# Gated recurrence with top-80 routing to eight experts: last loads on 128 partitions, zero writes in quarters, experts' products alternating, scatters without a chain

## The chip, the core and the metric

One core of a Trainium2 chip runs the whole program. Its engines are TensorE (PE in the rows; PEld is its weight load), VectorE (DVE), ScalarE (ACT), GpSimd (POOL) and SyncE (SP, which here only issues transfers); 16 DMA engines move data. The metric is device time in microseconds (us), the median of several executions. "The profiled execution" is one of them, and its span runs from its first to its last instruction.

## What is computed

Inputs are `x` and `f_logit` of shape (4, 5056, 256), a `lower_bound` of 256 values, `w_gate` (256, 8), `w1` (8, 256, 1024), `w2` (8, 1024, 256) and a capacity of 80; all are float32. Cut to what matters:

```python
sig = 1.0 / (1.0 + np.exp(-f_logit))
f = lower_bound + (1.0 - lower_bound) * sig
for t in range(S):                       # S = 5056, for each of 4 batches
    h = f[:, t] * h + (1.0 - f[:, t]) * x[:, t]
    y[:, t] = h
x = y.reshape(20224, 256)                # the tokens
logits = x @ w_gate                      # 8 experts
expert_idx = np.argmax(logits, axis=1)
gate_w = softmax(logits)[np.arange(N), expert_idx]
out = np.zeros((N, D))
for e in range(8):
    tok_idx = the (at most) 80 tokens of expert e with the largest gate_w
    h = np.maximum(x[tok_idx] @ w1[e], 0.0)
    out[tok_idx] = gate_w[tok_idx, None] * (h @ w2[e])
```

So 640 rows of the output hold values, and all others are zero.

## The kernel before, in words

**Stream.** The 5056 steps of a batch are cut into ten groups of 512 (the tenth has 448). A unit `n` is one batch of one group: 40 units, four to a group, batch by batch. For a unit, SP loads `f_t` and `x_t` (512 KB each; 448 KB on 112 partitions in the last group); ACT makes the sigmoid (`gate`); POOL multiplies it into `x_t` (`enter`); PE transposes both into channels by time (`to_channels`, tiles `sp` and `up`); ACT turns `sp` into the decay in the SBUF tensor `h_all` (`decay`); DVE runs the recurrence over time (`scan`, two halves of 128 channels); PE makes the gate logits (`lg`). The tile `up` has three PSUM buffers, of which a unit takes two. Once in four units a group's logits are copied (`aside`, `ls`), turned to tokens by PE (`lt`) and reduced by DVE (`maxima`, tiles `mx` and `cand`, then `choice`, tiles `eq` and `pick`). The loop over `n` issues the load of unit n+3, the gate of n+2, the transposes of n+1, the scan of n and the logits of n-1. Each engine works through its own list in the order in which the code was written.

**Zeros.** A 1 MB block of zeros in DRAM (`z_dram`) is copied over the output by SP. `clear` writes a piece; `zeros` lists the 160 pieces of 16 rows (128 KB; the last 8 have 96 KB). From unit 4 to unit 31 two pieces follow each unit's loads; 16 follow the last load, 40 go between and behind the first weights, 48 go with later weights.

**Selection.** After the stream every expert's candidates are reduced on all engines to a list of tokens (`vals`, `rank`, `put`, `kept`), which ends in `trow`, the token numbers.

**Experts.** Weights come in halves of 512 KB into a ring of six (`wring`); six halves are loaded ahead, the rest as halves are used up (`more`). For each expert, `gather` copies 80 columns of `h_all`, each by an instruction whose address comes out of a register: 24 on DVE, 32 on ACT, 24 on POOL, after one load of registers from `trow` per engine. `scaled` (tile `xt`), `hidden` (PE, `h_ps`), `relu` (ACT, `hid`), `result` (PE, `y_ps`), `finish` (DVE, `y`) follow, each for a whole expert. On PE the eight chunks of `hidden` for one expert stand ahead of the eight chunks of `result` for the one before it.

**Scatter.** `scatter` writes the 80 rows of `y` by an indirect DMA from POOL. All eight wait until the zero writes have landed, since they overwrite zeros, and each waits for the one before it to land, since both write `out`. SP's DMAs take eight semaphores in turn, so that each waits for the DMA eight places earlier to land.

The branch behind `doubt` (a full selection for rare ties) is not taken with these inputs.

Of the kernel before, what the change touches and what calls it, by code (L numbers as in the profile page):

```python
# [11 lines left out]
I32 = mybir.dt.int32  # L12
U32 = mybir.dt.uint32
# [4 lines left out]
P = 128  # L18
TOP = 8
AWAY = 1.0e6  # L20
PAD = 104
NONE = -64.0
GONE = -1.0e4
STEP = 128.0


@with_exitstack
def kernel(
# [25 lines left out]
    BESIDE = 4  # L54
# [13 lines left out]

    def tiles(ap, b, g):
        return ap[b, ds(first(g), size(g))].rearrange("(p r) d -> p r d", r=R)  # L70

    W = P // R
    assert B == R and C == R * R and all(size(g) % C == 0 for g in range(n_grp))
# [47 lines left out]
    NEW = DEEP + (n_grp - OLD) * P  # L121
# [3 lines left out]
    tops = consts.tile([P, NP, TOP], F32, name="tops")  # L125
    prev = consts.tile([P, 2 * TOP], F32, name="prev")
# [12 lines left out]
    h_all = hpool.tile([P, DC, N], F32, name="h_all")  # L139
# [8 lines left out]
    ZQ = 8  # L148
# [4 lines left out]
    def clear(k, q=None):  # L153
        n = min(ZR, N // P - k) * D
        rows = slice(0, P) if q is None else ds(q * QP, QP)
# [12 lines left out]
    def tokens(pool, at, ids):  # L168
# [5 lines left out]
        nc.vector.tensor_scalar(ids, parts[:, 0], float(S - R * W), spot_of[:, 0:1],  # L174
# [9 lines left out]
    psu = psum.enter_context(tc.tile_pool(name="psu", bufs=3, space=PSUM))  # L184
    plg = psum.enter_context(tc.tile_pool(name="plg", bufs=1, space=PSUM))

    with tc.tile_pool(name="ld", bufs=4) as ld, \
# [3 lines left out]

        def spot(n):
            g, b = divmod(n, B)
            return b * S + first(g)
# [40 lines left out]
        def load_f(n):  # L235
            g, b = divmod(n, B)
            fs[n] = ld.tile([P, R, D], F32, name="f_t", tag="f_t")
            nc.sync.dma_start(
                out=fs[n][:run(g)], in_=tiles(f_logit, b, g))

        def load_x(n):
            g, b = divmod(n, B)
            xs[n] = ld.tile([P, R, D], F32, name="x_t", tag="x_t")
            nc.sync.dma_start(
                out=xs[n][:run(g)], in_=tiles(x, b, g))

        def gate(n):
            s_t = sts[n] = fs.pop(n)[:run(n // B)]
            nc.scalar.activation(s_t, s_t, ACT.Sigmoid, scale=-1.0)  # L249

        def enter(n):
            u_t = uts[n] = xs.pop(n)[:run(n // B)]
            (nc.gpsimd if n else nc.vector).tensor_tensor(u_t, sts[n], u_t, ALU.mult)  # L253

        def to_channels(n, src, dst, pool, tag, in_time):
            k = run(n // B)
            for o in range(DC):
                ps = pool.tile([P, G], F32, name=tag, tag=tag)
                for r in range(R):
                    at = ps[:, r:R * k:R] if in_time else ps[:, ds(r * k, k)]  # L260
                    nc.tensor.transpose(at, src[n][:, r, ds(o * P, P)], ident[:k, :k])  # L261
                dst[n, o] = ps[:, :R * k]
            del src[n]

        def columns(n, o):
            return h_all[:, o, ds(spot(n), size(n // B))]
# [576 lines left out]
```

## Time and profile before

| | |
|---|---|
| median of 3 executions | 262.93 us (260.38 to 266.25) |
| the profiled execution, its own time | 260.38 us |
| its span | 258.6 us |
| busy: PE, DVE, ACT, POOL | 193.7, 160.7, 136.6, 136.4 us |
| moved by DMA | 81.13 MB, mean 314 GB/s |

Busy shares are means over stages with different limits, so the program has to be read stage by stage: the stream up to about 142 us, the selection up to about 163 us, the experts up to about 234 us, and the last scatters after that.

### The profile page before, as it was taken

Reading aid. Unit: us, or ns where it says so; the run is one execution under the profiler, and the core shown is the slowest. Engines: PE = TensorE matmul, PEld = TensorE weight load, DVE = VectorE, ACT = ScalarE, POOL = GpSimd, SP = SyncE. Lnnn points to the kernel's source line nnn. Section 1 sums busy time; section 2 is a strip of 40 time slices with the busy share of each in tenths; the row PEclk is TensorE's granted clock in tenths of the full one; section 3 lists DMA queues with packets and bytes.
Section 4 is the critical chain, followed back from the end, with each engine's and each line's share of the span. In section 5 each row is a group of like instructions: output and inputs, shape, how many; then the busy total and the mean of one; then the engine's idle time right before and its main releaser. Section 6 shows DMA issues by size and latency. Waiting matters only on the chain.

```text
span 258.6 us, 6254 instructions
## 1 busy us (share of the span) xinstructions
PE 193.7 (75%) x1841; PEld 159.1 (62%) x1841; DVE 160.7 (62%) x430; ACT 136.6 (53%) x430; POOL 136.4 (53%) x279
## 2 busy tenths in 40 slices
PE   1879989898889898988486758979999888882000
PEld 1757777676767676766364558868888657651000
DVE  4566988989898989897638488457555335000000
ACT  3657877676778787866744315465666551100000
POOL 2457878777777777776473710457444400012221
PEclk9997999999999999999979579999999999999555
DMA  6999999999999999999965888769999999961010
GB/s 190 402 418 416 421 415 426 414 416 417 420 414 415 418 414 420 414 370 274 297 212 161 286 273 297 205 202 340 324 351 371 345 354 362 326 249 35 20 31 15
DMA packets 30811, 81.13 MB, mean 314 GB/s; under 512 B 5040, under 2 KB 13360, under 8 KB 28336
## 3 DMA queue, kind: packets, MB, share of 16 engines
q1 hardware_dynamic: 29840, 79.97, 84.1%
q0 software_dynamic: 384, 0.66, 0.9%
q8 instruction: 17, 0.28, 0.4%
q14 instruction: 26, 0.21, 0.2%
q10 hardware_dynamic: 544, 0.01, 0.1%
HBM read 78.91 MB, written 22.41 MB: 392 GB/s over the span
## 4 chain that ended last, share of the span: by engine, by line
DMA 37%; PE 23%; DVE 12%; issue 8%; ACT 8%; SPq 6%; POOL 3%; ACTq 1%; POOLq 0%; DVEq 0%
DMA w_sb<-in_moe_w_dram 11%; DMA f_t<-in_f_logit_dram 10%; DMA x_t<-in_x_dram 8%; DVE h_all L278 6%; PE up L261 5%; PE h_ps L673 5%; PE sp L261 5%; DMA out_dram<-y,goal 5%; SPq L156 5%; PE lg L292 3%; ACT h_all L271 3%; PE y_ps L688 3%; DMA wg<-in_moe_w_gate_dram 2%; DVE eq L328 2%; ACT xe L655 2%
## 5 line engine op out<-in xcount | busy, mean ns | idle before, releaser
L253 POOL TENSOR_TENSOR x_t<-f_t,x_t 128x1024 f32<-128x1024 f32 (+1 forms) x39 | 92.3, 2369 | 32.6 <-DMA x_t<-in_x_dram 22.6
L278 DVE TENSOR_TENSOR_SCAN h_all<-h_all,up 128x512 f32<-128x512 f32 (+1 forms) x80 | 94.8, 1242 | 9.3 <-PE up L261 6.0
L249 ACT ACTIVATE f_t<-f_t 128x1024 f32<-128x1024 f32 (+1 forms) x40 | 42.4, 1059 | 31.9 <-DMA f_t<-in_f_logit_dram 31.9
L261 PE MATMUL up<-ident,x_t 128*128 128x128 f32 (+1 forms) x320 | 47.0, 287 | 13.6 <-DVE h_all L278 7.6
L271 ACT ACTIVATE h_all<-sp,nomlb 128x512 f32<-128x512 f32 (+1 forms) x80 | 49.9, 673 | 6.5 <-PE sp L261 6.3
L261 PE MATMUL sp<-ident,f_t 128*128 128x128 f32 (+1 forms) x320 | 46.0, 289 | 7.3 <-ACT f_t L249 5.8
L261 PEld LDWEIGHTS up<-ident,x_t 128*128 128x128 f32 (+1 forms) x320 | 37.2, 147 | 18.9 <-DVE h_all L278 8.4
L261 PEld LDWEIGHTS sp<-ident,f_t 128*128 128x128 f32 (+1 forms) x320 | 36.4, 147 | 15.8 <-issue 13.0
L655 POOL COPY xe<-h_all 128x2 f32 x192 | 23.9, 187 | 22.6 <-DVE xt L662 8.8
L655 ACT COPY xe<-h_all 128x2 f32 x256 | 25.4, 190 | 14.1 <-issue 10.6
L688 PE MATMUL y_ps<-w_sb,hid 128*80 128x256 f32 x128 | 29.3, 381 | 4.4 <-DMA w_sb<-in_moe_w_dram 2.9
L673 PE MATMUL h_ps<-xt,w_sb 128*128 128x80 f32 x256 | 30.0, 276 | 3.5 <-DMA w_sb<-in_moe_w_dram 1.8
L673 PEld LDWEIGHTS h_ps<-xt,w_sb 128*128 128x128 f32 x256 | 29.2, 192 | 5.1 <-PE y_ps L688 1.9
L292 PE MATMUL lg<-h_all,wg 128*32 128x128 f32 (+1 forms) x640 | 27.3, 288 | 6.1 <-ACT ls L300 4.5
L655 DVE COPY xe<-h_all 128x2 f32 x192 | 22.6, 172 | 12.5 <-issue 12.5
L697 POOL DMA_INDIRECT out_dram<-y,goal x8 | 7.5, 938 | 42.5 <-DMA w_sb<-in_moe_w_dram 25.8
L688 PEld LDWEIGHTS y_ps<-w_sb,hid 128*80 128x80 f32 x128 | 18.5, 150 | 13.0 <-ACT hid L681 4.8
L292 PEld LDWEIGHTS lg<-h_all,wg 128*32 128x32 f32 x640 | 15.8, 110 | 13.4 <-ACT ls L300 6.4
L694 DVE TENSOR_SCALAR y<-y_ps,gsl 80x256 f32<-80x256 f32 x8 | 3.8, 479 | 24.0 <-PE y_ps L688 24.0
L681 ACT ACTIVATE hid<-h_ps 128x320 f32<-128x320 f32 x16 | 6.6, 431 | 17.4 <-PE h_ps L673 17.4
L166 PEld LDWEIGHTS warm<-ident 128*128 128x128 f32 x92 | 12.5, 220 | 0.1
L166 PE MATMUL warm<-ident 128*128 128x128 f32 x92 | 12.5, 302 | 0.0
(125 smaller groups left out, 101.1 us busy)
## 6 DMA issues: line engine op xcount, KB each, us to landing
out_dram<-z_dram SPq DMA_DIRECT2D x152, 128.0 KB, 5.8
f_t<-in_f_logit_dram SPq DMA_DIRECT2D x36, 512.0 KB, 6.2
x_t<-in_x_dram SPq DMA_DIRECT2D x36, 512.0 KB, 6.2
w_sb<-in_moe_w_dram SPq DMA_DIRECT2D x32, 512.0 KB, 5.7
f_t<-in_f_logit_dram SPq DMA_DIRECT2D x4, 448.0 KB, 8.4
x_t<-in_x_dram SPq DMA_DIRECT2D x4, 448.0 KB, 9.7
z_dram<-zero SPq DMA_DIRECT2D x1, 1024.0 KB, 9.1
out_dram<-z_dram SPq DMA_DIRECT2D x8, 96.0 KB, 5.4
```

The source lines that it names most:

```text
L156: nc.sync.dma_start(out=out_z[rows, ds(k * D, n)], in_=z_dram[rows, :n])
L166: nc.tensor.matmul(warm, ident, ident, start=True, stop=True)
L249: nc.scalar.activation(s_t, s_t, ACT.Sigmoid, scale=-1.0)
L253: (nc.gpsimd if n else nc.vector).tensor_tensor(u_t, sts[n], u_t, ALU.mult)
L261: nc.tensor.transpose(at, src[n][:, r, ds(o * P, P)], ident[:k, :k])
L271: nc.scalar.activation(columns(n, o).rearrange("c (p r) -> c p r", r=R), sps.pop((n, o)).rearrange("c (r p) -> c p r", r=R), ACT.Identity, ...
L278: nc.vector.tensor_tensor_scan(h, h, ups.pop((n, o)), h_all[:, o, ds(spot(n) - 1, 1)] if n >= B else 0.0, ALU.mult, ALU.add)
L292: nc.tensor.matmul(lgs[g][ds(r * LC, LC), b, :k], wg[:, o], h[:, r], start=o == 0, stop=o == DC - 1, skip_group_check=True)
L655: copy(X[e][:, :, ds(k + j, 1)], h_all[:, :, ds(v, 1)])
L673: nc.tensor.matmul(h_ps[:, c], halves[i][:, o, ds(c * P, P)], xt[:, o], start=o == 0, stop=o == DC - 1, skip_group_check=True)
L688: nc.tensor.matmul(y_ps, hid[:, c], halves[c // CH][:, c % CH], start=c == 0, stop=c == FC - 1)
L697: nc.gpsimd.indirect_dma_start(out=out, out_offset=bass.IndirectOffsetOnAxis(ap=goal[:, ds(e, 1)], axis=0), in_=Y.pop(e), in_offset=None, ...
```

## The change

**Layout.** `h_all` becomes (batch, half, time), so that one batch's two halves lie 5056 columns apart. `trow` then holds byte addresses (4 times the column plus `HOME`, the address of `h_all`), and `rows_of` adds five small DVE operations that turn column numbers into output rows.

**Loads.** In the last group a load takes the last 512 steps of the batch (64 of them a second time) on 128 partitions; gate, product and transposes run on all 512, decay and scan on the new 448. The last unit's work is no longer moved ahead of its place. `up` gets four buffers; the selection's `ct` uses the buffers of `sp`.

**Zeros.** Pieces are quarters (32 rows, 256 KB), and neighbouring ones go out as one DMA of up to 1 MB: 14 in the loop, 6 after the last load, 30 among the first six weight halves, 30 with later ones (20 of 26 halves).

**Selection.** The second half of the early groups is summed on DVE (`sums`, `worth` on DVE for groups 6 and 7) instead of POOL; all 64 early maxima go into `fresh`, so that the last reductions are 320 wide instead of 268 and the reduction of the early ones alone goes; 16 warming matmuls go.

**Experts.** `gather` copies a token's two values as 2 x 4 bytes from a byte address, with no register arithmetic ahead of each copy (before: one register instruction ahead of each copy of 2 floats); 34 on DVE and 28 on ACT in two parts each, 18 on POOL; one `xt` product instead of two; on PE a chunk of `hidden` and the chunk of `result` six steps back alternate; weights come by halves in the order in which they are used.

**Scatter.** The scatters are declared independent of each other.

```diff
-        return ap[b, ds(first(g), size(g))].rearrange("(p r) d -> p r d", r=R)
+        return ap[b, ds(first(g) - lead(g), G)].rearrange("(p r) d -> p r d", r=R)
...
-    ZQ = 8
+    ZQ = 4
...
     def clear_some(m):
-        for k, q in zeros[:m]:
-            clear(k, q)
-        del zeros[:m]
+        while m > 0 and zeros:
+            k, q = zeros[0]
+            n = min(m, ZQ - q)
+            clear(k, q, n)
+            del zeros[:n]
+            m -= n
...
-    psu = psum.enter_context(tc.tile_pool(name="psu", bufs=3, space=PSUM))
+    psu = psum.enter_context(tc.tile_pool(name="psu", bufs=4, space=PSUM))
...
             if n + AHEAD == LAST:
-                clear_some(2 * ZQ)
-            elif B <= n < n_unit - 2 * B:
-                clear_some(2)
+                clear_some(6)
+            elif B <= n < n_unit - 2 * B and n % 2:
+                clear_some(1)
...
+        halved(0, HALF)
+        sums(HALF, OLD)
+        worth(0, 0, 2, nc.gpsimd)
+        candidates(0)
+        worth(OLD - 2, HALF, 2, nc.vector)
+        aside(g)
...
+    LAG = FC - 2
+    order = sorted(((which, e, i) for which in (1, 2) for e in range(E) for i in range(2)),
+                   key=lambda k: e_step(k, FC, CH, LAG))
+    RING = 6
...
-    for key in order[:3]:
+    for key in order[:RING]:
         w_sb[key] = weights(*key)
-        clear_some(ZQ)
-    clear_some(len(zeros) - BESIDE * (E - 2) * 2)
+        clear_some(5)
...
-    ways = [(mybir.EngineType.DVE, nc.vector.tensor_copy, 24),
-            (mybir.EngineType.Activation, nc.scalar.copy, 32),
-            (mybir.EngineType.Pool, nc.gpsimd.tensor_copy, K - 56)]
+    ways = [(mybir.EngineType.DVE, nc.vector.tensor_copy, [18, 16]),
+            (mybir.EngineType.Activation, nc.scalar.copy, [14, 14]),
+            (mybir.EngineType.Pool, nc.gpsimd.tensor_copy, [K - 62])]
...
+    h_bytes = h_all.rearrange("p b o s -> p (b o s)").bitcast(U8)
...
-                for o in range(DC):
-                    nc.vector.tensor_scalar_mul(XT[e][:, o], x_e[:, o], omlb[:, ds(o, 1)])
+                nc.vector.tensor_tensor(XT[e], X.pop(e),
+                                        omlb.unsqueeze(2).broadcast_to([P, DC, K]), ALU.mult)
...
-                    clear_some(BESIDE)
+                    clear_some(1 + len(late) % 2)
...
+            def steps(lo, hi):
+                for s in range(lo, hi):
+                    if s < E * FC:
+                        hidden(s)
+                    if 0 <= s - LAG < E * FC:
+                        result(s - LAG)
...
+                for other in sent:
+                    tc.declare_no_dep(one.ins, other.ins,
+                                      reason="a token is in one expert's list only")
+                sent.append(one)
...
+            for e in range(E):
+                s = e * FC
+                gather(e + 2, (0,))
+                steps(s, s + CH)
+                relu(e, 0)
+                gather(e + 2, (1,))
+                steps(s + CH, s + LAG)
+                if e > 0:
+                    finish(e - 1)
+                    scatters(e - 1)
+                elif not again:
+                    settle()
+                scaled(e + 2)
+                steps(s + LAG, s + FC)
+                relu(e, 1)
```

On SP the end of the stream stands like this before: loads of the last group, zero pieces (16 rows each) and the first weights.

```order
L238 DMA f_t<-in_f_logit_dram 112x1024
L244 DMA x_t<-in_x_dram 112x1024 x2
L156 DMA out_dram<-z_dram 16x2048 x16
L500 DMA w_sb<-in_moe_w_dram 128x2x512 x2
L156 DMA out_dram<-z_dram 16x2048 x8
L504 DMA w_sb<-in_moe_w_dram 128x4x256 x2
```

And like this after:

```order
L246 DMA f_t<-in_f_logit_dram 128x1024
L248 DMA x_t<-in_x_dram 128x1024
L164 DMA out_dram<-z_dram 64x2048
L164 DMA out_dram<-z_dram 128x2048
L490 DMA w_sb<-in_moe_w_dram 128x2x512
L164 DMA out_dram<-z_dram 128x2048
L164 DMA out_dram<-z_dram 32x2048
L490 DMA w_sb<-in_moe_w_dram 128x2x512
```

The same bytes of zeros take fewer and larger DMAs, and the weights go in one half at a time.

On POOL the last scatters stand like this before, with their waits (DMASW is the landing of an earlier scatter, DVE the tile `y`):

```order
L697 DMA out_dram<-y,goal 20224x256 [waits DMASW3_49,DVE_49]
L697 DMA out_dram<-y,goal 20224x256 [waits DMASW4_49,DVE_49]
L697 DMA out_dram<-y,goal 20224x256 [waits DMASW5_49,DVE_49]
L697 DMA out_dram<-y,goal 20224x256 [waits DMASW6_49,DVE_49]
```

And all eight like this after (DMAHW is the landing of the zeros and loads):

```order
L734 DMA out_dram<-y,goal 20224x256 [waits DMAHW4_49,DMAHW5_49,DMAHW3_49,DMAHW6_49,DMAHW2_49,DMAHW7_49,DMAHW1_49,DMAHW0_49]
L734 DMA out_dram<-y,goal 20224x256 x2
L734 DMA out_dram<-y,goal 20224x256 [waits DVE_49] x5
```

The first still waits for the zeros; none waits for another scatter.

## Rows read from the trace of the kernel before

**Rows 1.** Busy by stretch (PE, PEld, DVE, ACT, POOL), granted clock, DMA share, GB/s.

```profile
98.35:110.80 12.45, 10.93 (x140) 8.93 (x136) 11.43 (x13) 9.50 (x13) 9.56 (x6) 1.00 1.02 418
...
114.60:126.50 11.90, 9.91 (x126) 7.86 (x124) 10.14 (x13) 8.69 (x13) 5.79 (x3) 1.00 1.04 267
...
139.00:162.50 23.50, 16.53 (x141) 13.78 (x135) 16.95 (x59) 6.90 (x24) 8.04 (x21) 0.78 0.84 274
162.50:174.00 11.50, 9.04 (x77) 8.70 (x78) 6.73 (x53) 7.14 (x67) 6.22 (x50) 1.00 0.67 192
...
204.00:229.90 25.90, 21.55 (x142) 17.68 (x143) 7.48 (x54) 6.54 (x46) 0.13 (x2) 1.00 1.00 350
```

**Rows 2.** Timeline of DVE: start, length, operation, idle before it and its releaser.

```profile
33.38 0.29 DVE L318 TENSOR_REDUCE mx<-lt 128x16 f32<-128x128 f32 x1 [1.50 <-PE lt L306]
...
108.10 0.29 DVE L318 TENSOR_REDUCE mx<-lt 128x16 f32<-128x128 f32 x1 [0.95 <-PE lt L306]
108.42 0.29 DVE L319 TENSOR_TENSOR cand<-lt,mx 128x128 f32<-128x128 f32 x1
...
112.55 0.29 DVE L332 TENSOR_REDUCE pick<-eq 128x16 f32<-128x128 f32 x1
...
139.15 0.27 DVE L328 SCALAR_TENSOR_TENSOR eq<-cand,revexp 128x128 f32<-128x128 f32 x1
...
139.66 2.18 DVE L278 TENSOR_TENSOR_SCAN h_all<-h_all,up 128x448 f32<-128x448 f32 x2
```

**Rows 3.** Groups by line from 60 to 110 us: busy, mean ns, idle before.

```profile
L278 DVE TENSOR_TENSOR_SCAN h_all<-h_all,up 128x512 f32<-128x512 f32 x33 | 39.5, 1259 | 0.0
...
L261 PE MATMUL up<-ident,x_t 128*128 128x128 f32 x128 | 18.2, 277 | 4.0 <-DVE h_all L278 4.0
...
L328 DVE SCALAR_TENSOR_TENSOR eq<-cand,revexp 128x128 f32<-128x128 f32 x4 | 5.1, 1286 | 0.0
```

**Rows 4.** DMA issues of the whole program: KB each, median us to landing.

```profile
f_t<-in_f_logit_dram SPq DMA_DIRECT2D x36, 512.0 KB, 6.2
...
f_t<-in_f_logit_dram SPq DMA_DIRECT2D x4, 448.0 KB, 8.4
```

**Rows 5.** Timeline from the end of the selection on, all engines and SP's issues.

```profile
157.90 13.99 SPq L156 DMA_DIRECT2D out_dram<-z_dram  x19
...
162.48 0.23 DVE L604 CAST trow<-kept 8x80 int32<-8x80 f32 x1 [1.33 <-PE kept L601]
...
165.13 3.13 ACT L655 COPY xe<-h_all 128x2 f32 x32 [2.17 <-issue]
...
168.66 3.80 PE L673 MATMUL h_ps<-xt,w_sb 128*128 128x80 f32 x32 [1.11 <-DVE xt L662]
...
170.19 2.81 DVE L655 COPY xe<-h_all 128x2 f32 x24 [1.41 <-issue]
171.99 1.04 SPq L500 DMA_DIRECT2D w_sb<-in_moe_w_dram  x2
...
173.81 3.68 PE L688 MATMUL y_ps<-w_sb,hid 128*80 128x256 f32 x16 [1.35 <-ACT hid L681]
```

**Rows 6.** Register loads of the gather: ns shortest, median, longest.

```profile
L651 DVEq TENSOR_LOAD <-trow x8: 1601/1604/1860, 162.7 to 212.5; - x8
L651 ACTq TENSOR_LOAD <-trow x8: 1954/1974/2169, 162.8 to 208.2; - x8
```

**Rows 7.** The gather's copies on DVE, as a group (page, part 5).

```profile
L655 DVE COPY xe<-h_all 128x2 f32 x192 | 22.6, 172 | 12.5 <-issue 12.5
```

**Rows 8.** The end: the chain's last weight transfer.

```profile
224.88 4.94 DMA w_sb<-in_moe_w_dram
```

**Rows 9.** The end: timeline after the last weight.

```profile
234.44 0.48 DVE L694 TENSOR_SCALAR y<-y_ps,gsl 80x256 f32<-80x256 f32 x1 [3.30 <-PE y_ps L688]
...
253.26 0.91 POOL L697 DMA_INDIRECT out_dram<-y,goal x1 [2.17 <-DMA out_dram<-y,goal]
```

**Rows 10.** The end: the table of waits.

```profile
POOL out_dram L697 <- DMA out_dram<-y,goal: 16.7, 7, 3.1
```

More of the change, by code (lines that the diff above doesn't have):

```diff
@@ L24, with e_step @@
 STEP = 128.0
+WORD = 4
+HOME = 67552
+def e_step(key, chunks, half, lag):
+    which, e, i = key
+    return e * chunks + i * half + (lag if which == 2 else 0), which
 @with_exitstack
@@ L405 @@
         LAST = n_unit - 1
-        done_f = []
         for n in range(-AHEAD, n_unit):
-            m = n + AHEAD
-            for k in (m, m + 1):
-                if k < n_unit and k not in done_f and (k == m or m >= LAST - 2):
-                    done_f.append(k)
-                    load_f(k)
-            unit(load_x, m)
+            unit(load, n + AHEAD)
             if n == -1:
@@ L529, in slots_down @@
         weigh(sp[:, ds(E, E)])
[L530 removed]
+        rows_of(sp[:, :E], far)
     doubts = consts.tile([P, 6], F32, name="doubts")
@@ L642, in experts @@
             w = {} if again else w_sb
-            late = list(order if again else order[3:])
-            X, XT, HID, Y = {}, {}, {}, {}
-            def gather(e):
-                X[e] = xp.tile([P, DC, K], F32, name="xe", tag="xe")
-                k = 0
-                for engine, copy, n in ways:
-                    _, at_tok = nc.values_load_multi_w_load_instructions(
-                        trow[ds(e, 1), ds(k, n)], engines=(engine,), min_val=0, max_val=N - 1,
-                        skip_runtime_bounds_check_because="token numbers come from iota")
-                    for j, v in enumerate(at_tok):
-                        copy(X[e][:, :, ds(k + j, 1)], h_all[:, :, ds(v, 1)])
-                    k += n
+            late = list(order if again else order[RING:])
@@ new lines, in experts, with pair, gather @@
+            X, XT, HP, HID, YP, Y = {}, {}, {}, {}, {}, {}
+            def pair(at):
+                one = h_bytes[:, ds(at, WORD)]
+                return bass.AP(one.tensor, one.offset, [one.ap[0], (WORD * S, DC), one.ap[1]])
+            def gather(e, parts):
+                if e >= E:
+                    return
+                if 0 in parts:
+                    X[e] = xp.tile([P, DC, K], F32, name="xe", tag="xe")
+                xe = X[e].bitcast(U8)
+                k = 0
+                for engine, copy, ns in ways:
+                    for i, n in enumerate(ns):
+                        if i in parts:
+                            _, at_tok = nc.values_load_multi_w_load_instructions(
+                                trow[ds(e, 1), ds(k, n)], engines=(engine,),
+                                min_val=HOME, max_val=HOME + SPAN,
+                                skip_runtime_bounds_check_because="token numbers come from iota")
+                            for j, v in enumerate(at_tok):
+                                copy(xe[:, :, ds(WORD * (k + j), WORD)],
+                                     pair(v - HOME))
+                        k += n
@@ L679, in relu @@
-            def relu(e, ps):
-                for i in range(2):
-                    nc.scalar.activation(HID[e][:, ds(i * CH, CH)], ps[i], ACT.Relu)
-            def result(e):
-                y_ps = psy.tile([K, D], F32, name="y_ps", tag="y_ps")
-                halves = w.pop((2, e))
-                hid = HID.pop(e)
-                for c in range(FC):
-                    nc.tensor.matmul(y_ps, hid[:, c], halves[c // CH][:, c % CH],
-                                     start=c == 0, stop=c == FC - 1)
-                return y_ps
```

275 lines of the change are left out of this document (125 added, 150 removed).

## The prediction

> **What bounds the kernel now.** I read the stretches first [rows 1], then the engine that ends last in each. In a middle group of the stream (98.35 to 110.80 us) the DMA engines are full (share 1.02, 418 GB/s) and DVE is busy for 11.43 of 12.45 us; the maxima of groups 0 and 6 start at 33.38 and 108.10 us, six periods of 12.45 [rows 2]. A period moves four units' loads (4.19 MB) and eight zero pieces (1.05 MB): 5.24 MB at 418 GB/s are 12.5 us, so the transfers set it. The compute side is close behind: PE waits 4.0 us in four groups for a scan to free a buffer of `up` [rows 3], and DVE then waits 0.95 us for `lt` [rows 2].
>
> In the last group the share stays at 1.04 while the rate falls to 267 GB/s [rows 1], and a 448 KB load lands after 8.4 us where 512 KB take 6.2 [rows 4]: a load on 112 partitions costs the engines more than a larger one on 128. The last scan ends at 139.66 + 2.18 = 141.84 us [rows 2].
>
> The selection runs to 162.71 us, the end of `trow` [rows 5]. From 162.5 to 174.0 the DMA share is only 0.67 [rows 1], with SP still issuing zeros until 171.89, 0.74 us for each 128 KB [rows 5]. The first refill of the weight ring goes out at 171.99, and the last weight lands at 224.88 + 4.94 = 229.82 [rows 5, 8]. In between the DMA share is about 1 (1.00 at 350 GB/s at the end [rows 1]): the expert stage is set by its bytes. Then come 24.2 us, from the last `y` at 234.44 to the end of the span at 258.6, in which POOL's eight scatters go one after another; seven wait 16.7 us for the landing of the one before [rows 9, 10].
>
> **The change, part by part.** The sum is made against the profiled execution, 260.38 us with a span of 258.6; it is the lowest of the three shown, whose median is 2.55 higher.
>
> *Stream.* The loop sends 14 quarters (3.67 MB) where it sent 56 eighths (7.34 MB). A period then moves 4.19 + 0.52 MB, 11.3 us at 418 GB/s. DVE's 11.43 us of work don't shrink, and become the bound; the fourth `up` buffer takes away PE's wait, 1.0 us per group. PE's own 10.93 plus other short waits could hold the period above DVE's work. I take 11.7; the ends are 11.43 (nothing but DVE) and 12.45 (a chain through the engines that I don't see keeps it). Seven periods put the maxima of group 7 at 33.38 + 81.9 = 115.3. From there DVE has the two reductions (0.58), a scan of 512 (2 x 1.26), `eq` and `pick` (1.29 + 0.29), four units of 448 (4 x 2.18) and one more set of reductions, 0.58 + 0.56: 14.5 us [rows 2, 3]. With all loads on 128 partitions at 418 GB/s four units take 10.0 us of transfer, less than that, so DVE stays the bound and the last scan ends at 129.8: **-12.0** (with 12.45 for the period -6.8, with 11.43 -13.9). The 64 repeated steps cost ACT's sigmoid and POOL's product nothing here: both take as long on 112 partitions as on 128, and both engines have slack (9.5 and 9.6 of 12.45 [rows 1]).
>
> *Selection.* From last scan to `trow` it took 20.9 us. POOL has one halving less (it goes to DVE), but the exponentials now stand behind the last unit's decay on ACT, so POOL's chain starts later against the last scan; the early maxima's own reduction goes, and three reductions are 320 wide instead of 268. I take **+0.5**, ends -2 and +2.
>
> One row speaks for a price on DVE: `eq`, with two SBUF inputs, takes 0.27 us when POOL is idle and 1.29 beside POOL's products [rows 2, 3]. The Trainium skill has this as a rule (SBUF — State Buffer, "Who interferes with whom"): a VectorE instruction with two SBUF inputs and a GpSimd one that reads SBUF exclude each other for their whole length. The change moves two such products (`worth` for groups 6 and 7) from POOL to DVE beside POOL's chain, and makes `xt` one. By the rule, with `eq`'s price, the selection's term would be 2 x (1.29 - 0.27) = 2.0 higher, which is its upper end; by the row of an idle POOL it stays. The trace agrees with the rule, and shows no operation of this kind beside POOL's short ones.
>
> *Start of the experts.* A register load lasts 1.60 us for 24 registers and 1.97 for 32 [rows 6]: 0.046 for each and 0.50 fixed, so 1.14 for 14, 1.33 for 18. Splitting adds 0.3 to 1.0 per expert and engine. The copies stand 0.117 us apart on DVE (24 in 2.81) and 0.098 on ACT (32 in 3.13) with a register instruction ahead of each [rows 5]; without it less, with 8 one-byte elements instead of 2 words more. No row shows a byte copy: below, half of today's spacing (0.06) because an engine instruction is left for each; above, no overlap at all, the 172 ns that one lasts [rows 7]. I take 0.09. A later load overlaps with the copies ahead of it by 0.2 (1.60 long, 1.41 idle [rows 5, 6]). Expert 0's copies on DVE then end 0.45 + 1.33 + 18 x 0.09 + 1.03 + 16 x 0.09 = 5.9 us after `trow`, and `hidden` starts after 6.2, nearly as before (168.66 - 162.71 = 5.95). ACT does 70 copies and five loads ahead of its first `relu` (before 64 and two): 0.45 + 5 x 1.14 - 0.8 + 70 x 0.09 = 11.7 us, and PE, which now stops at step 6 of the alternation for it, goes on at 12.1 (before: 173.81, 11.1). The ring's first half is free at +8, the second only with step 7, at +13.9.
>
> *Expert stage.* The loaded-ahead halves and 30 quarters need 29 us of transfer (6 x 1.65 + 7.86 x 2.45, prices below) from about 127 on, when the last unit's products leave their tiles ahead of its scan, so they are through near 156, 5 us after `trow`; merged DMAs of up to 1 MB end SP's limit. Before, 26 halves and 48 pieces (6.03 MB) took 57.83 us from 171.99 to 229.82. At the stream's price of 2.45 us per MB (1.02 / 418 GB/s) the zeros are 14.8 of it, so a half is 43.0 / 26 = 1.65. After the second refill there remain 25 halves and 29 quarters (7.34 MB): 41.4 + 18.0 = 59.4, so the last weight lands 73.3 after `trow` where it was 67.1: **+6.2**. The ends: -2 (the ring never runs dry, quick copies) and +5 (copies at 0.17).
>
> PE is not the bound: `hidden` takes 3.80 us and `result` 3.68 per expert [rows 5], 0.46 per chunk each, 0.92 per step if alternation gains nothing, 7.4 per expert, against 10.2 of transfer while zeros run. Over the last six halves without zeros (9.9 us) PE needs 12 steps, about 10.5, so it ends some 3.2 after the last landing where it took 4.6 to the last `y`: **-1.4**.
>
> *End.* With zeros gone from the ring after 20 of 26 refills, five scatters go out some ten us ahead of the end, the next two as their `y` comes. After the last product there are one `y` (0.48), 0.1 and a scatter to the end of the span, 258.6 - 253.26 = 5.34 [rows 9]: 5.9 instead of 24.16, **-18.2**. If POOL were still busy with the scatter before (0.91), +1. The five small operations of `rows_of` lie in DVE's slack while expert 2 is gathered.
>
> Sum: -12.0 + 0.5 + 6.2 - 1.4 - 18.2 = -24.9, a span of 233.7, an execution of 235.5. Since the profiled execution was the lowest of three, I say **236**.
>
> **The rivals.**
> *The stream keeps its period* (12.45), held by the compute chain: +5.2, 241. For it: DVE and PE are at 92 and 88% already. Against: PE's wait for `up` is the one that repeats in every group, and the fourth buffer ends it. It lies inside the range. 0.15.
> *The ring never runs dry* and the copies are quick: the last weight 7 earlier, 229. For it: the copies lose an instruction each. Against: ACT's five loads ahead of the first `relu`. 0.12.
> *The change doesn't do what it says at the end:* without a declared order the scatters are still served one at a time, 3.08 apart as now, with two in front of the last: +6.2, 242; with all eight held until the last zeros land late, 254. Against: the chain's rows show waits on landings, not POOL's 0.91 of work. 0.05.
> *The register loads cost more than the fit:* if a load lasts as long as the longest of today, 2.17 us [rows 6], however few registers it takes, ACT's five ahead of the first `relu` take 10.9 us instead of 5.7, and all behind it comes 5.2 later, 241. Against: the medians differ with the count. 0.01. The Trainium skill has a dearer rule (Runtime: NRT & Kernel Launch, "Instruction fetch mechanics": about 200 ns for each register); by it the 70 registers would take 14.0 us and the result would be an estimated 244, but the row of 1.97 us for 32 registers, which would have to be 6.4, speaks against it.
> *Slower than before:* the byte copies bind DVE. An expert costs it two loads (2.56), 34 copies, a `y` (0.48) and an `xt` (taken like `pick`, 0.29); eight of them, then the last expert's 14 steps (12.9) and the end (5.9), from `trow` at 151.2: 196.6 us plus 272 times one copy. That passes the old span of 258.6 from 0.228 us a copy on, and 2% more from 0.247. A copy lasts 0.172 today [rows 7], so copies without any overlap give 243; beyond 0.228 a byte copy would have to last a third longer than a word copy. 0.06 for binding at all, 0.02 of it slower than before.
>
> **How the numbers follow.** My own sum with its smaller errors (228 to 243) has 0.61. The range reaches from the second rival's 227 to 246, which takes in the stream's rival with the selection's and the copies' upper ends; it leaves out the binding copies, the held scatters and the far ends of several terms at once. A change of 2%, about what a measurement of this kernel can tell from none, is 257.7 or 268.2 here: faster 0.95, within 2% 0.03, slower 0.02.
>
> **What would show it.** Period: DVE's maxima 11.4 to 11.9 us apart, with no wait of PE for `up`. Last group: 128-partition loads landing in about 6 us and about 418 GB/s, last scan near 130. Selection: `trow` near 151. Gather: spacing of copies on DVE between 0.06 and 0.12. Experts: DMA share near 1 from 14 us after `trow`, last weight near 224.5. End: the last scatter about 1 us after the last product, with no wait for another one. I would be wrong if the period stays at 12.45, if byte copies stand more than 0.17 apart, or if the expert stage turns out to be bound by PE rather than by its bytes.

## The result, and the profile after

| | before | after |
|---|---|---|
| median of 4 executions | 264.0 us | 234.55 us (233.3 to 235.15) |
| ratio, 95% interval | | 0.8958 (0.8856 to 0.906) |
| profiled execution, span | 260.38, 258.6 us | 233.3, 231.5 us |
| end of the last scan | 141.84 | 126.07 |
| end of `trow` | 162.71 | 148.05 |
| start of the last `y` | 234.44 | 225.29 |

The change saves 29 us in the medians and 27.1 in the profiled executions. The stretches of the changed kernel (columns as in [rows 1]):

```profile
78.10:89.36 11.26, 10.74 (x136) 8.98 (x139) 10.94 (x12) 9.43 (x14) 9.82 (x6) 1.00 1.02 418
...
111.80:126.10 14.30, 12.16 (x172) 9.76 (x172) 13.85 (x19) 10.08 (x15) 8.84 (x7) 1.00 0.70 276
126.10:148.05 21.95, 13.32 (x87) 11.36 (x88) 15.20 (x51) 6.67 (x24) 5.69 (x18) 0.69 1.01 372
148.05:158.00 9.95, 6.73 (x55) 6.54 (x54) 3.42 (x39) 4.64 (x43) 2.77 (x22) 0.93 0.56 226
158.00:166.00 8.00, 7.19 (x31) 6.41 (x31) 3.64 (x43) 5.10 (x44) 4.57 (x34) 0.50 0.30 101
...
200.00:212.00 12.00, 10.29 (x67) 7.93 (x65) 5.27 (x54) 4.13 (x31) 0.00 (x0) 1.00 1.04 405
212.00:225.30 13.30, 13.12 (x84) 10.67 (x84) 0.97 (x3) 1.39 (x4) 6.60 (x7) 1.00 0.75 268
```

A group of the stream takes 11.2 us where it took 12.45, with DVE busy for 10.94 of it. In the last group DVE is busy for 13.85 of 14.30 and the DMA engines are not full any more. The new hole is at 148 to 166 us: the share falls to 0.56 and 0.30 while the experts start. From 212 on PE is idle for 0.18 us in all.

The clock column has a second hole. TensorE's granted clock is 0.50, the lower of its two levels (1.2 instead of 2.4 GHz), from 156.7 to 166.9 us. Just before, PE had stood idle for 3.22 us, and its first 24 products take 4.93 us (timeline):

```profile
156.11 4.93 PE L701 MATMUL h_ps<-xt,w_sb 128*128 128x80 f32 x24 [3.22 <-DVE xt L677]
```

The timeline of DVE shows the same places:

```profile
100.54 0.29 DVE L322 TENSOR_REDUCE mx<-lt 128x16 f32<-128x128 f32 x1 [0.17 <-PE lt L310]
...
103.43 0.74 DVE L332 SCALAR_TENSOR_TENSOR eq<-cand,revexp 128x128 f32<-128x128 f32 x1
...
123.90 2.17 DVE L281 TENSOR_TENSOR_SCAN h_all<-h_all,up 128x448 f32<-128x448 f32 x2
...
126.69 0.68 DVE L371 TENSOR_TENSOR gm<-marks,sm 128x128 f32<-128x128 bf16 x2
...
147.82 0.23 DVE L605 TENSOR_SCALAR trow<-kept 8x80 int32<-8x80 f32 x1 [1.33 <-PE kept L602]
150.00 1.41 DVE L669 COPY xe<-h_all 128x8 uint8 x18 [1.95 <-issue]
154.27 1.33 DVE L669 COPY xe<-h_all 128x8 uint8 x16 [2.86 <-issue]
```

The wait for `lt` is down from 0.95 to 0.17 us. Sixteen byte copies take 1.33 us, 0.083 each, but DVE stands still for 2.86 us ahead of its second part, and does so again for every expert. The register loads (as [rows 6]) say why:

```profile
L664 DVEq TENSOR_LOAD <-trow x16: 1568/2719/3640, 148.1 to 206.3; - x16
L664 ACTq TENSOR_LOAD <-trow x16: 1216/2138/3230, 148.1 to 203.0; - x16
L664 POOLq TENSOR_LOAD <-trow x8: 4038/4054/4249, 148.1 to 189.7; - x8
```

POOL's 18 registers take 4.05 us, where 24 took 1.57 before:

```profile
L651 POOLq TENSOR_LOAD <-trow x8: 1542/1566/1772, 162.7 to 196.7; - x8
```

And the end, POOL's timeline:

```profile
213.89 1.12 POOL L734 DMA_INDIRECT out_dram<-y,goal  x1 [15.23 <-DMA w_sb<-in_moe_w_dram]
215.32 0.91 POOL L734 DMA_INDIRECT out_dram<-y,goal  x1 [0.30 <-issue]
...
226.04 0.91 POOL L734 DMA_INDIRECT out_dram<-y,goal  x1 [1.77 <-DVE y L731]
```

The scatters start when the zeros have landed and go out 1.2 us apart; the last comes 0.75 us after the start of its `y`, where it came 18.8 us after it [rows 9].

### The profile page after: what moved, and what is told of

Read it like the earlier page. It is cut to its first block, busy times and chain, and to the rows that moved or that the text cites. A ratio compares the mean times of both kernels' runs of the same rounds, so it can differ in the third digit from the quotient of the medians.

```text
span 231.5 us, 5464 instructions
## 1 busy us (share of the span) xinstructions
PE 191.3 (83%) x1825; PEld 160.9 (69%) x1825; DVE 156.0 (67%) x503; ACT 134.4 (58%) x399; POOL 130.6 (56%) x229
## 2 busy tenths in 40 slices
DMA packets 29188, 81.58 MB, mean 352 GB/s; under 512 B 3296, under 2 KB 11616, under 8 KB 26720
## 4 chain that ended last, share of the span: by engine, by line
DMA 38%; PE 28%; ACT 10%; DVE 7%; issue 6%; POOL 5%; DVEq 2%; ACTq 0%; POOLq 0%; SPq 0%
DMA f_t<-in_f_logit_dram 17%; DMA out_dram<-z_dram 7%; PE sp L263 7%; DMA w_sb<-in_moe_w_dram 7%; PE y_ps L716 5%; PE lg L296 5%; ACT h_all L273 4%; DMA x_t<-in_x_dram 4%; DVE xe L669 4%; PE up L263 3%; PE h_ps L701 3%; POOL x_t L256 3%; DMA wg<-in_moe_w_gate_dram 3%; ACT f_t L252 3%; PE warm L178 2%
## 5 line engine op out<-in xcount | busy, mean ns | idle before, releaser
L256 POOL TENSOR_TENSOR x_t<-f_t,x_t 128x1024 f32<-128x1024 f32 x39 | 92.3, 2375 | 19.4 <-DMA x_t<-in_x_dram 16.1
L263 PE MATMUL sp<-ident,f_t 128*128 128x128 f32 x320 | 46.1, 289 | 7.0 <-ACT f_t L252 5.8
L701 PEld LDWEIGHTS h_ps<-xt,w_sb 128*128 128x128 f32 x256 | 40.3, 208 | 14.1 <-DVE xt L677 4.5
L252 ACT ACTIVATE f_t<-f_t 128x1024 f32<-128x1024 f32 x40 | 42.5, 1062 | 12.1 <-DMA f_t<-in_f_logit_dram 12.1
L263 PE MATMUL up<-ident,x_t 128*128 128x128 f32 x320 | 43.6, 281 | 4.3 <-POOL x_t L256 2.6
L263 PEld LDWEIGHTS sp<-ident,f_t 128*128 128x128 f32 x320 | 36.5, 146 | 15.1 <-issue 12.5
L669 DVE COPY xe<-h_all 128x8 uint8 x272 | 22.0, 164 | 34.6 <-issue 34.6
L263 PEld LDWEIGHTS up<-ident,x_t 128*128 128x128 f32 x320 | 37.1, 144 | 6.6 <-POOL x_t L256 4.5
L669 POOL COPY xe<-h_all 128x8 uint8 x144 | 19.4, 195 | 36.6 <-issue 17.8
L669 ACT COPY xe<-h_all 128x8 uint8 x224 | 23.7, 193 | 23.7 <-issue 23.5
L296 PEld LDWEIGHTS lg<-h_all,wg 128*32 128x32 f32 x640 | 15.6, 109 | 11.7 <-ACT ls L304 4.8
```

The lines of the kernel that those rows point to most:

```text
L263: nc.tensor.transpose(at, src[n][:, r, ds(o * P, P)], ident)
L296: nc.tensor.matmul(lgs[g][ds(r * LC, LC), b, :k], wg[:, o], h[:, r], start=o == 0, stop=o == DC - 1, skip_group_check=True)
L669: copy(xe[:, :, ds(WORD * (k + j), WORD)], pair(v - HOME))
L701: nc.tensor.matmul(HP[e, i][:, c], w[1, e, i][:, o, ds(c * P, P)], XT[e][:, o], start=o == 0, stop=o == DC - 1, skip_group_check=True)
```

## The experiments

Medians are compared by their ratio to the kernel before, timed on the same chip. "One execution" is a single one, whose time is no surer than the 1 to 2% by which those of one kernel differ; it was made for its trace.

### What makes a register load slow

In `trow` a part starts at four bytes times the number of tokens ahead of it. Before, that was 0, 96 and 224; after, 0 and 72 on DVE, 136 and 192 on ACT, 248 on POOL.

```diff
-    ways = [(mybir.EngineType.DVE, nc.vector.tensor_copy, [18, 16]),
-            (mybir.EngineType.Activation, nc.scalar.copy, [14, 14]),
-            (mybir.EngineType.Pool, nc.gpsimd.tensor_copy, [K - 62])]
+    ways = [(mybir.EngineType.DVE, nc.vector.tensor_copy, [16, 16]),
+            (mybir.EngineType.Activation, nc.scalar.copy, [16, 16]),
+            (mybir.EngineType.Pool, nc.gpsimd.tensor_copy, [K - 64])]
```

> The changed kernel with the gather split 16+16 on DVE, 16+16 on ACT and 16 on POOL (instead of 18+16, 14+14, 18), so that every register load starts at a multiple of 64 bytes of its row. Theory A (the start address sets the price: in the changed kernel the loads that start at 72, 136 and 248 bytes are the slow ones, about 0.22 us a register, those at 0 and 192 bytes the quick ones): every load takes about 0.5 + 16 x 0.046 = 1.2 us, DVE's wait ahead of the second part falls from 2.86 us to under 1.0, the first product of expert 0 starts 5 to 6.5 us after the token list instead of 8.1, and the time falls by 2 to 5 us from 234.6. Theory B (it is the second load, or three engines loading at once, that costs): medians of the loads stay at 2 to 4 us, the start stays at +8 and the time within 1 us of 234.6.

Measured: 227.85 us, ratio 0.868 (0.8619 to 0.8742), well under the change's 0.8958. All forty loads are quick:

```profile
L664 DVEq TENSOR_LOAD <-trow x16: 1095/1100/1356, 147.7 to 193.1; - x16
L664 ACTq TENSOR_LOAD <-trow x16: 1007/1022/1217, 147.7 to 195.4; - x16
L664 POOLq TENSOR_LOAD <-trow x8: 1049/1064/1283, 147.7 to 174.2; - x8
```

and the first product starts 5.2 us after `trow`, with DVE idle for 0.40 us ahead of its second part (timeline):

```profile
150.87 1.32 DVE L669 COPY xe<-h_all 128x8 uint8 x16 [0.40 <-issue]
...
152.90 2.90 PE L701 MATMUL h_ps<-xt,w_sb 128*128 128x80 f32 x24 [0.34 <-DVE xt L677]
```

Theory A. The time falls by 6.7 us, more than the 2 to 5 expected: the granted clock also stays at 1.00 through the whole expert stage, and the first 24 products take 2.90 us where they took 4.93. What the clock alone is worth was not measured. The second kernel makes the same loads slow in the kernel before, which has one load per engine:

```diff
-    ways = [(mybir.EngineType.DVE, nc.vector.tensor_copy, 24),
-            (mybir.EngineType.Activation, nc.scalar.copy, 32),
-            (mybir.EngineType.Pool, nc.gpsimd.tensor_copy, K - 56)]
+    ways = [(mybir.EngineType.DVE, nc.vector.tensor_copy, 20),
+            (mybir.EngineType.Activation, nc.scalar.copy, 30),
+            (mybir.EngineType.Pool, nc.gpsimd.tensor_copy, K - 50)]
```

> The kernel before with its gather split 20 on DVE, 30 on ACT, 30 on POOL instead of 24, 32, 24: loads then start at byte 0, 80 and 200 of the row instead of 0, 96 and 224. Theory A (start address): POOL's load of 30, at 200 bytes, takes 30 x 0.22 = 6.6 us instead of 1.57 for 24; ACT's of 30, at 80 bytes, takes 1.9 us if a multiple of 16 bytes is enough and 6.6 if it takes more; DVE's takes 1.4. Theory B (a second load or bunching): all stay on the line 0.50 + 0.046 a register: 1.4, 1.9, 1.9 us. The time is of less interest: with A some 5 us more than before in the start of the experts, with B none.

One execution: 282.74 us, against 262.67 for the kernel before.

```profile
L651 POOLq TENSOR_LOAD <-trow x8: 6673/6711/6881, 165.2 to 237.6; - x8
L651 DVEq TENSOR_LOAD <-trow x8: 1349/1355/1609, 165.2 to 240.5; - x8
L651 ACTq TENSOR_LOAD <-trow x8: 2165/2183/2343, 165.2 to 234.8; - x8
```

The time rises by 20 us, where some 5 were expected, because the dear load, and 30 copies of POOL instead of 24, come again for every expert: DVE's `xt` waits for POOL's copies eight times, 42.8 us in all. POOL's load at byte 200 takes 6.71 us, 0.224 per register; ACT's at byte 80 takes 2.18, near the quick price. So starts at 0, 80, 96, 192 and 224 are quick, and those at 200 and 248 (and, by DVE's and ACT's longest, 72 and 136) slow. A multiple of 16 bytes fits all of them. Neither the second load nor three engines loading at once is to blame.

### The scatters

```diff
-                for other in sent:
-                    tc.declare_no_dep(one.ins, other.ins,
-                                      reason="a token is in one expert's list only")
-                sent.append(one)
```

> The changed kernel with the scatters in their old order, each waiting for the one before to land. Theory A (the chain costs 3.08 us for each as before): first scatter at 213.9 when the zeros have landed, the eighth 7 x 3.08 later at 235.5, span 240.8, time +9 us from 234.6. Theory B (the zeros' earlier end did most of it, and only the scatters near the end queue): the last two only, +3 us.

Measured: 247.47 us, ratio 0.9428 (0.9354 to 0.9501), 12.9 more than the change. Theory A, and dearer than expected; the table of waits (us in total, times, longest):

```profile
POOL out_dram L734 <- DMA out_dram<-y,goal: 20.3, 7, 5.2
```

Before, seven waits made 16.7 [rows 10]. Here the first scatters leave while weights still fill the DMA engines, and the first landing is waited for 5.2 us. The other way round, the kernel before with the scatters declared independent:

> The kernel before with one edit: the scatters declared independent. Theory A (they still wait for all zeros, to about 229.9, and then go out 1.22 us apart): eighth scatter at about 238.5, span 244, 14.6 us less than before, ratio 0.944. Theory B (without the order the chip still serves them one at a time, 3.08 apart): no change. The rest of the change would then be worth 264.0 - 234.6 - 14.6 = 14.8 us by theory A.

Measured: 247.19 us against 264.5, ratio 0.9343 (0.9289 to 0.9397), 17 us less and more than theory A's 14.6. POOL's timeline, whose last `y` starts at 238.97:

```profile
233.93 1.12 POOL L697 DMA_INDIRECT out_dram<-y,goal  x1 [27.16 <-DMA w_sb<-in_moe_w_dram]
235.35 0.92 POOL L697 DMA_INDIRECT out_dram<-y,goal  x1 [0.31 <-issue]
...
242.66 0.91 POOL L697 DMA_INDIRECT out_dram<-y,goal  x1 [0.30 <-POOLq L769]
```

The chip does not serve them one at a time: from the start of the last `y` to the end of the span it takes 8.0 us, where it took 24.2. Made first, this one edit is 17 of the 29 us, and the rest of the change takes the time from 247 to 234.55; taken out of the changed kernel it is worth 12.9, so what it is worth depends on the rest.

### The stream: zeros, the buffer, the partitions

```diff
-                clear_some(6)
-            elif B <= n < n_unit - 2 * B and n % 2:
-                clear_some(1)
+                clear_some(20)
```

> The changed kernel with no zero pieces in the loop; the 14 quarters go out behind the last load instead. A period then moves 4.19 MB. Theory A (transfers set the period of 11.19): 4.19 / 0.42 = 10.0 us. Theory B (DVE sets it: 10.84 busy of 11.19): 10.8 to 11.0. Theory C (a chain through PE, ACT and POOL): 11.2 as now. DVE's maxima give the period. The time is not the point, since the zeros come back later.

One execution, 233.13 us. Two groups of the stream:

```profile
66.69:77.74 11.05, 10.54 (x136) 8.99 (x139) 10.46 (x12) 9.34 (x14) 9.85 (x6) 1.00 1.00 386
77.74:88.80 11.06, 10.54 (x136) 9.01 (x139) 10.46 (x12) 9.33 (x14) 9.80 (x6) 1.00 1.02 393
```

With 11% fewer bytes the period only goes from 11.2 to 11.05, so theory A's 10.0 falls. This does not show that transfers no longer set the period of the changed kernel, only that another bound lies close below. Waits in five groups of the changed kernel, and then in five of this one:

```profile
POOL x_t L256 <- DMA x_t<-in_x_dram: 3.9, 7, 0.7
ACT f_t L252 <- DMA f_t<-in_f_logit_dram: 3.7, 10, 0.5
```
```profile
DVE mx L322 <- PE lt L310: 2.6, 5, 0.5
PE lg L296 <- ACT ls L304: 2.6, 5, 0.5
```

In the changed kernel ACT and POOL still wait for loads, the chain that ended last lies for more than half of these groups in loads of `f_t`, and the 4.72 MB of a period need 11.3 us at its 418 GB/s: by these rows transfers set its period. Without the zeros nothing waits for a load. PE works for 10.54 us of a period and waits 0.52 for ACT's `ls`, which makes up the 11.05; DVE works for 10.46 and waits for PE. That is theory C's chain, and it ends last in PE, not in DVE. The DMA share stays at 1.0 at 386 GB/s, so a full share alone does not show that transfers set the pace.

```diff
-    psu = psum.enter_context(tc.tile_pool(name="psu", bufs=4, space=PSUM))
+    psu = psum.enter_context(tc.tile_pool(name="psu", bufs=3, space=PSUM))
```

> The changed kernel with three buffers of `up` instead of four. Theory A (the fourth buffer took away a wait of 1.0 us per group of four units, and DVE is now the bound): PE waits for a scan again, DVE's maxima stand 11.6 to 12.2 us apart instead of 11.19, the last scan ends 4 to 7 us later, the time 237 to 241. Theory B (fewer zeros alone shortened the period): 11.2 as now.

One execution, 235.48 us. The maxima of groups 2 to 7 stand 11.48 us apart ((113.64 - 56.23) / 5) instead of 11.21 and the last scan ends 1.8 us later, between the two theories, and DVE waits for `lt` again (groups by line, 55 to 113 us; the second row is the changed kernel's):

```profile
L322 DVE TENSOR_REDUCE mx<-lt 128x16 f32<-128x128 f32 x5 | 1.5, 292 | 4.8 <-PE lt L310 4.8
```
```profile
L322 DVE TENSOR_REDUCE mx<-lt 128x16 f32<-128x128 f32 x6 | 1.7, 292 | 1.8 <-PE lt L310 1.8
```

The buffer is thus worth 0.3 us of a period. By the sums the other 0.97 came with half the zeros per group; the kernel before with half its zeros was not run.

```diff
-            nc.sync.dma_start(out=fs[n], in_=tiles(f_logit, b, g))
+            nc.sync.dma_start(out=fs[n][:run(g)], in_=tiles(f_logit, b, g))
...
-            s_t = sts[n] = fs.pop(n)
+            s_t = sts[n] = fs.pop(n)[:run(n // B)]
```

> The changed kernel with the last group's loads on 112 partitions again (448 KB, no repeated steps, products and transposes on 112). Theory A (these loads cost the DMA engines more: 3.67 MB at 267 GB/s are 13.7 us where 4.19 MB at 418 were 10.0): the last scan ends 2 to 4 us later against the maxima of group 7 than the 14.26 of the changed kernel. Theory B (DVE was busy for 13.85 of the last 14.3 us, so the loads are hidden): within 0.5 us, nothing gained by the 128 partitions once the zeros are fewer.

One execution, 238.59 us; the last scan ends at 130.63 instead of 126.07. DVE's timeline in the last group:

```profile
112.68 0.29 DVE L323 TENSOR_REDUCE mx<-lt 128x16 f32<-128x128 f32 x1 [1.18 <-PE lt L311]
...
120.26 2.18 DVE L282 TENSOR_TENSOR_SCAN h_all<-h_all,up 128x448 f32<-128x448 f32 x2 [2.02 <-ACT h_all L274]
125.33 0.29 DVE L323 TENSOR_REDUCE mx<-lt 128x16 f32<-128x128 f32 x1 [2.88 <-PE lt L311]
...
128.46 2.17 DVE L282 TENSOR_TENSOR_SCAN h_all<-h_all,up 128x448 f32<-128x448 f32 x2
```

Theory A: from the maxima of group 7 to the last scan's end it takes 17.95 us instead of 14.26, with waits of DVE that the changed kernel doesn't have. Loading 64 steps twice on 128 partitions saves 3.7 us here (and 0.9 just ahead of it). An `f_t` of 448 KB lands after 10.2 us (median), one of 512 KB after 6.7. The page counts the same 3296 packets under 512 B in both kernels, so small packets are not the cause; the cause stays open.

### Byte addresses and alternation

```diff
-    nc.vector.tensor_scalar(trow, flat_p[:E], float(WORD), float(HOME), ALU.mult, ALU.add)
+    nc.vector.tensor_scalar(trow, flat_p[:E], 1.0, 0.0, ALU.mult, ALU.add)
...
-    copy(xe[:, :, ds(WORD * (k + j), WORD)], pair(v - HOME))
+    copy(xe[:, :, ds(k + j, 1)], pair(v))
```

> The changed kernel with the byte addresses undone alone: `trow` holds column numbers and a copy takes two 4-byte words, with a register instruction ahead of each. Theory A (that instruction sets the spacing of copies): 0.117 us on DVE and 0.098 to 0.105 on ACT as before the change, instead of 0.081 and 0.105; DVE's 34 copies of an expert take 1.2 us longer, the first product comes 1 to 1.5 us later after the token list than 8.1, the time rises by 1 to 3 us. Theory B (the copies hide behind the slow loads, 2.86 us idle): the spacing rises but the time stays within 0.5.

Measured: 250.58 us, ratio 0.9495 (0.9419 to 0.957): 16 us more than the change, far beyond both theories. DVE's timeline:

```profile
149.72 2.12 DVE L669 COPY xe<-h_all 128x2 f32 x18 [2.02 <-issue]
...
155.98 1.77 DVE L669 COPY xe<-h_all 128x2 f32 x15 [0.32 <-issue]
...
165.40 1.89 DVE L669 COPY xe<-h_all 128x2 f32 x16 [3.63 <-issue]
```

The spacing is 0.118, as theory A says. What both lacked is the load behind the copies: DVE idles 3.63 us instead of 2.86 ahead of its second part. By my reading the load starts later, since the copies' register instructions stand ahead of it until the last copy; that was not tried by itself; the loads themselves last as long as in the changed kernel (2.71 us on DVE, median). Two loads and 34 copies then make DVE the bound: its `xt` come some 10 us apart (189.89, 199.43, 209.36, 219.49 and 229.88) where PE needs 6.7 for eight steps. Part of the 16 us is the clock's, and how much was not separated: behind its waits PE's granted clock is 0.50, for instance from 192 to 196 us, behind 4.14 us of idling. That DVE binds is the prediction's mechanism for a slower kernel, brought about by dear loads instead of dear copies.

```diff
                 for s in range(lo, hi):
                     if s < E * FC:
                         hidden(s)
+                for s in range(lo, hi):
                     if 0 <= s - LAG < E * FC:
```

> The changed kernel with PE's products not alternating: within each half expert (4, 2 and 2 steps) the chunks of `hidden` stand together, then those of `result`; the order of the weights is the same. Theory A (alternation shortens a step from 0.92 to 0.837, but the stage up to about 212 us waits for transfers): steps at 0.92, of which only the last 14 to 16 count, +1.2 us. Theory B (the alternation sets the stage): 64 steps of 0.083 more, +5. Theory C (the pair costs the same in any order): step 0.84 and no change.

Measured: 235.17 us, ratio 0.8929 (0.8842 to 0.9016), no difference from the change. Without waits a step takes 0.855 in pairs (from 213.04 to 214.75) and 0.877 in fours, against 0.837. So alternation gains 0.02 to 0.04 a step here; theory C comes nearest.

### The idle DMA engines

```diff
-        clear_some(5)
+        clear_some(7)
```

> The changed kernel with seven zero quarters behind each of the first six weight halves instead of five, so that 12 quarters (3.1 MB) fewer are left for the refills. Theory A (the DMA engines stand nearly idle for some 10 us around the start of the experts, and are the bound from about 188 to 212 us): 12 x 0.26 MB x 2.45 us = 7.7 us of transfer move into the idle stretch, the share there rises from 0.2 to 0.5 to near 1, PE stops waiting for weights, and the time falls by 4 to 8 us from 234.6. Theory B (the expert stage follows PE and the gather, transfers only seem full): less than 1 us. Theory C (the zeros stand in the refill's way): the first refill lands later and the time rises by 1 to 3 us.

Measured: 233.63 us, ratio 0.89 (0.8835 to 0.8966), no difference that can be told: theory B. The gather still sets the pace: its `xt` on DVE come 8 us apart (196.77, 205.15, 212.92), and DVE waits for nothing between them but its register loads. So the same edit was made with the loads aligned and the scatters held back:

```diff
-                if not zeros:
+                if not zeros and e >= E - 4:
```

> The changed kernel with three edits: register loads aligned (16+16, 16+16, 16), seven zero quarters behind each of the first six weight halves instead of five, and the scatters held back until the last expert's gather stands ahead of them on POOL. Theory A (with the early zeros alone the gain was lost because POOL, waiting for the zeros ahead of its first scatter at 196.7, held up the gathers behind it; without that, PE is the bound): first product 5.4 us after the token list, then 64 steps of 0.837 and six of 0.46 = 56.4 plus some 3 of waits, last y at about 212.5, span about 218.6, time 220.5, some 7 below the 227.9 of the aligned loads alone. Theory B (the zeros' place doesn't matter, the weights' own transfers set the stage): 227 to 228 as with the aligned loads alone.

Measured: 226.52 us, ratio 0.8584 (0.8527 to 0.8642), an interval that overlaps that of the aligned loads: theory A's 220.5 falls. The hole at 148 is filled (share 1.01 and 0.99), but PE still waits for weights, and behind one such wait its granted clock is 0.50 from 168 to 171.4 us (timeline):

```profile
167.39 0.63 PE L716 MATMUL y_ps<-w_sb,hid 128*80 128x256 f32 x2 [1.96 <-DMA w_sb<-in_moe_w_dram]
```

And the DMA engines also idle ahead of the first weights, which wait for the stream's tiles (stretches):

```profile
119.00:122.00 3.00, 2.92 (x36) 2.62 (x37) 2.65 (x5) 0.93 (x3) 2.35 (x2) 1.00 0.31 126
122.00:125.00 3.00, 2.04 (x43) 1.62 (x40) 2.97 (x6) 2.97 (x4) 0.41 (x1) 1.00 0.18 50
```

```diff
             if n + AHEAD == LAST:
-                clear_some(6)
+                clear_some(14)
...
         w_sb[key] = weights(*key)
-        clear_some(7)
+        clear_some(6)
```

> The combined kernel with its zeros shifted once more: 14 quarters behind the last load instead of 6, then six behind each of the first six weight halves instead of seven, 16 left for the refills. Theory A (the DMA engines are now the bound of everything behind the stream, and the combined kernel still leaves them nearly idle from 119.5 to 124.5 us, shares 0.31 and 0.18): 8 quarters fit into that hole, some 4 us of transfer, and the time falls from 226.5 to 222 to 223. Theory B (the first weights only go out later behind the zeros, or something other than transfers holds PE): 226 to 228.

Measured: **223.19 us**, ratio 0.8463 (0.8394 to 0.8532), 11 below the change and the best of all. The same stretches, and the last ones:

```profile
119.00:122.00 3.00, 2.99 (x37) 2.69 (x38) 2.66 (x5) 0.93 (x3) 2.28 (x1) 1.00 1.02 366
122.00:125.00 3.00, 2.03 (x46) 1.61 (x48) 2.97 (x6) 2.97 (x4) 0.41 (x1) 1.00 1.01 352
...
180.00:200.00 20.00, 18.76 (x129) 15.99 (x129) 7.76 (x72) 10.66 (x86) 6.97 (x21) 1.00 1.02 370
200.00:215.00 15.00, 15.00 (x102) 12.60 (x100) 0.96 (x2) 1.75 (x4) 1.82 (x2) 1.00 0.64 217
```

Near the 222 to 223 of theory A. The two intervals still touch, but all four times lie below all four of the combined kernel (223.07 to 223.93 against 225.75 to 227.88), and the trace shows a reason: PE waits for no weight longer than 0.44 us, and its clock stays at 1.00 through the experts. PE is now busy for 33.8 of the 35 us up to 215, so moving more zeros has little left to win.

## Why the prediction was right

The forecast was 236 and the result 234.55. The end and the last group of the stream were read rightly; for the rest luck has a part in how near it came. The terms, against the profiled executions:

| term | predicted | measured |
|---|---|---|
| to the end of the last scan | -12.0 | -15.8 |
| selection | +0.5 | +1.1 |
| `trow` to the last `y` (+6.2 - 1.4) | +4.8 | +5.5 |
| end | -18.2 | -17.95 |
| sum | -24.9 | -27.1 |

The stream gained 3.8 us more than its term, the other three lost 1.6 against theirs, and the median of the four executions lies 1.25 above the profiled one.

*Stream.* The step that failed is "DVE's 11.43 us of work don't shrink, and become the bound". DVE's work shrank to 10.94, the period is 11.2 instead of 11.7 and below the lower end of 11.43, and what sets it by the rows above is the transfers, whose 11.3 us the prediction had worked out itself; PE's chain (11.05) and DVE (10.94) lie close below. DVE's work shrank because `eq` takes 0.27 to 0.75 us in the middle groups where it took 1.29 [rows 3]. The trace shows why. At 103.43 it starts inside a product of POOL that ends at 104.03, and ends 0.14 later; in the kernel without zeros in the loop it starts at 69.58, just behind a product that ends at 69.57, and takes 0.27; before, at 110.99 inside one that ended at 112.37, it took 1.53 (POOL's product in the changed kernel; then POOL's and `eq` before):

```profile
101.65 2.38 POOL L256 TENSOR_TENSOR x_t<-f_t,x_t 128x1024 f32<-128x1024 f32 x1 [0.73 <-DMA x_t<-in_x_dram]
```
```profile
110.00 2.37 POOL L253 TENSOR_TENSOR x_t<-f_t,x_t 128x1024 f32<-128x1024 f32 x1 [1.05 <-ACT h_all L271]
110.99 1.53 DVE L328 SCALAR_TENSOR_TENSOR eq<-cand,revexp 128x128 f32<-128x128 f32 x1
```

It waits for what is left of POOL's product. That is the Trainium skill's rule (SBUF — State Buffer, "Who interferes with whom"), and the trace agrees with it. I had held the old 1.29 fixed, though it was a matter of phase. The last group went as reasoned: DVE is busy for 13.8 of its 14.26 us, 14.5 were forecast, and the 128 partitions are worth 3.7 by their own experiment.

*Selection.* The two products that moved to DVE took 0.68 us together, not 2 x 1.29: the price from `eq` was rightly left at the end of the range.

*Start of the experts.* This step failed in its working. The copies were right (0.083 on DVE for 0.09; ACT 0.105), but loads were put at 0.50 + 0.046 per register by rows that all started at multiples of 32 bytes. In the changed kernel three of five start elsewhere. The first product came 8.1 us after `trow` instead of 6.2 and the second refill 17.3 instead of 13.9. The prediction also priced PE's products by rows at a granted clock of 1.00 [rows 1]; here it was 0.50 for ten us behind the wait. The Trainium skill's price (Runtime: NRT & Kernel Launch, "Instruction fetch mechanics", about 200 ns per register), stated there for loads that the runtime injects, fits the slow loads, at 0.224, and not the quick ones. I gave that rival 0.01, because the row of 32 registers spoke against it; the row was true, but only of its address.

*Expert stage.* The error hardly showed, because another of about its size lay against it, and that was luck. Transfers were priced at 59.4 us behind the second refill. The DMA share falls at about 220.5, so they took some 55; the windows up to 212 show 405 GB/s where the old stage ended at 350 [rows 1]. PE then needed some 5 us from there to the last `y` where 3.2 were predicted. The stage is bound by its bytes for a part only: the chain that ended last runs through DVE's gather up to 173.6 us, through transfers from 179 to 212, and through PE from there on. That alternation gains little, as allowed for with 0.92 a step, was right in its effect.

*End.* Right to 0.3 us: the first scatter goes out 12 us ahead of the last, six go out together (five were forecast), and none waits for another. The rival that the chip serves scatters one at a time is ruled out.

## What to carry to other kernels

Chained writes at a program's end cost their full latency each: where they can't overlap, declare them independent (13 to 17 us of 29 here). A price taken from rows holds for the addresses and phases of those rows: when a change moves a load's start or one engine's work against another's, ask what the old number depended on. Where TensorE is made to wait, look at its granted clock behind the wait: here waits of 2 and 3 us were followed by 3 and 10 us at half of it. And when a resource is full in one stretch and idle in the next, look for work without a deadline, like the zeros here, to move into every hole; it pays only once no other engine is the bound.

## What the runs showed of the hardware

- A load of 16 registers takes 1.02 to 1.10 us (0.07 each) from bytes 0, 64, 128, 192 or 256 of the row; from bytes 200 and 248 it costs 0.224 for each (30 in 6.71, 18 in 4.05). Byte 80 is quick (30 in 2.18).
- A copy of 128 x 8 bytes lasts as long as one of 128 x 2 words (164 and 172 ns on DVE), so byte addresses, which need no arithmetic, cost nothing there; without the register instruction ahead of each, DVE's copies stand 0.083 us apart instead of 0.118.
- TensorE's granted clock was 0.50 from 156.7 to 166.9 us in the changed kernel, behind 3.22 us of idling, and 24 products took 4.93 us; at 1.00, in the kernel with aligned loads, they took 2.90.
- The DMA share stood at 1.0 at 386 GB/s and at 418 GB/s in the same loop.
- In the last group, 448 KB loads on 112 partitions move 269 GB/s at a share of 0.93, with as few small packets as the 128-partition loads.
